# Row transposes of the second batch placed later, three ReLUs moved from ScalarE to VectorE, and transforms of later batches placed slightly earlier, in a retention + Fourier-mix + feed-forward kernel

## The chip, the cores and the metric

One core of a Trainium2 chip runs the whole kernel. The metric is device time of one execution in microseconds (us), median of several executions. A profiled execution also gives a span (first to last instruction, some 1.8 to 2.1 us less than the device time) and a record of every instruction. Batches, row blocks and hidden blocks are counted from 0: batch 1 is the second batch.

## The reference, cut to what matters

Four batches of 768 rows and 512 columns. Retention attention with a decaying state per head gives `x`; then a Fourier mix, a normalisation and a two-layer network:

```python
# q, k, v: (4, 8, 768, 64); w_ch1: 512 x 2048; w_ch2: 2048 x 512
state = gamma * state + k[t] (x) v[t]          # per head, over 768 steps
x[t]  = scale * q[t] @ state
u  = x + real(fft(fft(x, axis=1), axis=2))     # rows, then columns
un = (u - mean(u)) / sqrt(var(u) + 1e-6)
out = u + max(un @ w_ch1, 0) @ w_ch2
```

## The kernel before

The kernel works with two halves of 384 rows per batch; a row block is 128 rows. The feed-forward part of batch b is the bulk of TensorE's work. Woven between its units is the attention of batch b+1 and the mix of the next row half. The parts that the argument needs (cuts marked with `# ...`):

```python
ACT_ROWS = ((2, 4, 5, 6, 7, 8, 9, 10, 14), (0, 3, 6, 7, 9, 10, 11, 12, 14, 15), (2, 4, 5, 6, 7, 8, 9, 10, 14))

def h_unit(b, rt, fb):                    # hidden block fb of 16, row half rt
    psh = ps_pm.tile(...)                 # one of 3 PSUM buffers
    for cb in range(4):
        nc.tensor.matmul(psh, w116[...], unT[...])            # 4 x 384 columns
    if fb in ACT_ROWS[2 if (b, rt) == (B - 1, 0) else rt]:
        nc.scalar.activation(ht16[:, fb, :], psh, AF.Relu, ...)
    else:
        nc.vector.tensor_scalar(out=ht16[:, fb, :], in0=psh, ...)   # ReLU too

# second transform of row block kb ("pq"), from its unit:
pq = ps_g.tile(...)                       # the PSUM pool that wkK, wkA, wkY, pst use too
# ... 4 matmuls into pq
nc.scalar.copy(qn..., pq...)              # twice (L829, L830)
nc.vector.scalar_tensor_tensor(out=u[:, kb, 0:256], in0=lo, ...)     # L834, reads pq
nc.vector.scalar_tensor_tensor(out=u[:, kb, 256:512], in0=updn, ...) # L837, reads pq
nc.gpsimd.tensor_tensor(out=u[:, kb, 0:256], ...)       # + x, L864
nc.gpsimd.tensor_tensor(out=u[:, kb, 256:512], ...)     # + x, L866
nc.vector.bn_stats(bst, u[:, kb, :])                    # L883
# ... mean, then un = u - mean on ScalarE (L885)

def unT_unit(b, kb):                      # transposed rows, for h_unit
    if b > 1 or b and kb >= 3:
        nc.sync.dma_start_transpose(unT[...], un)       # by DMA
        return
    # else 4 transposes on TensorE ("pst"), copy on VectorE or ScalarE
```

Where a unit goes in the order is set by numbers, in fractions of a batch's work. A list of units is spread evenly between a start and an end, all lists are merged by that place, and a scheduler builds the final order for each engine from it:

```python
dm = (0.12, 0.24, 0.3, 0.38) if b == 0 else (0.004, 0.140, 0.232, 0.341)
streams += [(majors, b, b + 1.0), (s2s, b + dm[0], b + dm[1]),   # pq of row blocks 3 to 5
            (unTs, b + dm[2], b + dm[3])]                        # their transposes
# ... attention of batch b+1, ending at `end`
da = (0.062, 0.080, 0.173, 0.203, 0.255, 0.305) if b == 0 else \
    (0.068, 0.072, 0.053, 0.163, 0.173, 0.194)
streams.append((s1 units of b+1, end + da[0], end + da[1]))      # first transform
s2s, unTs = mix_units(b + 1, [0, 1, 2])
streams += [(s2s, end + da[2], end + da[3]), (unTs, end + da[4], end + da[5])]
```

## Time and profile before

| | before |
|---|---|
| device time, median of 3 | 248.96 us (248.73 to 249.09) |
| span of the profiled execution | 247.2 us |
| TensorE waits outside the start-up, turn to batch 1 / 2 / 3 | 2.01 / 1.11 / 1.20 us |

The last row is worked out in the prediction. From the list of waits of TensorE (engine, what waited and its line, what released it: total us, times, longest), two lines of the turns:

```profile
PE wkY L644 <- DVE u L837: 0.8, 2, 0.4
...
PE pst L914 <- ACT un L885: 0.4, 1, 0.4
```

These are gaps as shown; what a gap costs beyond that is worked out in the prediction. In timelines, a line is: start, length from first start to last end, engine, line, operation, output<-input, shape, count, and in brackets the gap before it with what ended it. PE is TensorE, DVE VectorE, ACT ScalarE and POOL GpSimd; L644 is line 644 of the kernel. The prediction explains most names; besides them, v is the cast of v to 16 bits, s the state update of the attention, atm its mask product, bst and stats the row statistics, and ob the output.

### The profile page before, as it was taken

What the parts mean: (1) busy time and instruction counts of PE and PEld (TensorE: products, weight loads), DVE (VectorE), ACT (ScalarE), POOL (GpSimd) and SP (SyncE); (2) the same over time, 40 slices, a digit from 0 to 9 for tenths busy, and PEclk for the clock granted to TensorE, in tenths of its full rate; (3) what the DMA queues carried; (4) which work ended last, traced back from release to release, by engine and by line L of the source; (5) the groups of instructions that cost most, each with busy time, mean ns of one, the idle gap of its engine ahead of it and who ended that gap; (6) DMA issues with size and microseconds to landing.
All of it is one profiled execution on the core that took longest, in us unless ns stands there. A gap on an engine that the chain in (4) does not pass through costs nothing.

```text
span 247.2 us, 5308 instructions
## 1 busy us (share of the span) xinstructions
PE 234.4 (95%) x2024; PEld 144.2 (58%) x2024; DVE 176.5 (71%) x427; ACT 124.8 (50%) x279; POOL 81.6 (33%) x146
## 2 busy tenths in 40 slices
PE   6797899999999999999999999999999998999994
PEld 2454668956776645665567546555666455445543
DVE  8988957898788787897885748787895656424112
ACT  8798678487786434651247515632257317202500
POOL 7668500385500075690000636760002314000000
PEclk9999999999999999999999999999999999999999
DMA  8999999699999288979999468685200241221012
GB/s 174 258 258 148 197 198 203 154 245 261 280 225 219 46 170 195 205 146 139 263 271 201 98 153 199 117 137 127 81 0 3 49 143 23 44 85 42 0 45 85
DMA packets 99209, 36.39 MB, mean 147 GB/s; under 512 B 89840, under 2 KB 96240, under 8 KB 99184
## 3 DMA queue, kind: packets, MB, share of 16 engines
q1 hardware_dynamic: 94960, 31.86, 61.4%
q0 software_dynamic: 4224, 4.19, 10.5%
q8 instruction: 16, 0.26, 0.4%
q14 instruction: 9, 0.07, 0.1%
HBM read 27.26 MB, written 6.29 MB: 136 GB/s over the span
## 4 chain that ended last, share of the span: by engine, by line
PE 66%; DVE 10%; POOL 8%; ACT 6%; SPq 3%; issue 2%; DMA 2%; POOLq 0%; DVEq 0%; ACTq 0%
PE psc L973 30%; PE psh L930 19%; PE ps L730 3%; SPq L159 3%; PE psh L947 3%; DVE bst L883 3%; POOL u L866 2%; DMA k<-in_k_dram 2%; POOL u L864 2%; PE wkA L594 2%; PE wkY L648 2%; DVE u L834 1%; DVE ht L936 1%; PE wkY L644 1%; PE tq L550 1%
## 5 line engine op out<-in xcount | busy, mean ns | idle before, releaser
L973 PE MATMUL psc<-w,ht 128*128 128x512 f16 (+1 forms) x400 | 89.8, 370 | 0.1
L930 PE MATMUL psh<-unT,w 128*128 128x384 f16 x448 | 81.9, 326 | 0.8 <-ACT ht L934 0.6
L973 PEld LDWEIGHTS <-ht 128*128 128x128 f16 x400 | 38.0, 98 | 35.3 <-issue 0.3
L930 PEld LDWEIGHTS <-w 128*128 128x128 f16 x448 | 42.2, 98 | 24.8 <-issue 2.0
L934 ACT ACTIVATE ht<-psh 128x384 f16<-128x384 f32 x67 | 31.6, 488 | 37.9 <-PE psh L930 37.1
L864 POOL TENSOR_TENSOR u<-u,x 128x256 f32<-128x256 f32 x21 | 13.3, 636 | 102.6 <-DVE u L834 92.2
L977 DVE SCALAR_TENSOR_TENSOR ob<-psc,stats,u 128x512 f32<-128x512 f32 (+1 forms) x25 | 18.1, 722 | 26.8 <-PE psc L973 26.7
L936 DVE TENSOR_SCALAR ht<-psh 128x384 f16<-128x384 f32 x45 | 24.7, 551 | 8.5 <-PE psh L930 7.9
L597 DVE TENSOR_TENSOR atm<-wkA,maskp 128x512 f16<-128x512 f32 x36 | 23.9, 683 | 1.0 <-PE wkA L594 1.0
L885 ACT ACTIVATE un<-u,stats 128x512 f16<-128x512 f32 x21 | 15.1, 721 | 18.5 <-DVE stats L884 14.8
L883 DVE BATCH_NORM_STATS2 bst<-u 128x6 f32<-128x512 f32 x21 | 14.6, 695 | 10.7 <-POOL u L866 10.5
L623 DVE SCALAR_TENSOR_TENSOR s<-s,gk,wkK 128x128 f16<-128x128 f16 x48 | 16.4, 342 | 2.5 <-ACT s L619 1.4
L656 ACT ACTIVATE x<-wkY,gexp 128x384 f16<-128x384 f32 x24 | 12.9, 581 | 8.3 <-PE wkY L648 8.3
L377 POOL TENSOR_SCALAR kd<-k,gexp 128x384 f16<-128x384 f32 x24 | 13.8, 587 | 2.5 <-DMA k<-in_k_dram 2.5
L145 PE MATMUL wps<-ht 128*128 128x512 f16 x40 | 12.6, 419 | 2.2 <-POOL ht L196 2.2
L866 POOL TENSOR_TENSOR u<-u,x 128x256 f32<-128x256 f32 x21 | 13.4, 636 | 3.6 <-DVE stats L884 1.8
L594 PE MATMUL wkA<-qTz,kT 128*128 128x256 f16 x72 | 13.6, 273 | 0.0
L829 ACT COPY qn<-pq 128x128 f32<-128x128 f32 x18 | 5.0, 275 | 14.6 <-PE pq L827 14.6
L947 PE MATMUL psh<-unT,w 128*128 128x128 f16 x192 | 11.5, 219 | 0.1
L947 PEld LDWEIGHTS <-w 128*128 128x128 f16 x192 | 11.1, 98 | 0.7 <-issue 0.5
L382 POOL TENSOR_SCALAR v<-v 128x768 f16<-128x768 f32 x12 | 10.0, 833 | 2.0 <-DMA v<-in_v_dram 1.9
L594 PEld LDWEIGHTS <-kT 128*128 128x128 f16 x72 | 6.9, 98 | 6.0 <-DVE s L623 0.4
(164 smaller groups left out, 318.8 us busy)
## 6 DMA issues: line engine op xcount, KB each, us to landing
q<-in_q_dram SPq DMA_DIRECT2D x16, 384.0 KB, 6.2
k<-in_k_dram SPq DMA_DIRECT2D x16, 384.0 KB, 5.6
v<-in_v_dram SPq DMA_DIRECT2D x16, 384.0 KB, 6.4
out_dram<-ob SPq DMA_DIRECT2D x23, 256.0 KB, 2.6
w<-in_moe_w_ch_dram POOLq DMA_DIRECT2D x8, 512.0 KB, 11.0
out_dram<-ob SPq DMA_DIRECT2D x2, 128.0 KB, 1.7
unT<-un SPq DMA_TRANSPOSE x15, 2.4
qTz<-q16z SPq DMA_TRANSPOSE x8, 3.8
```

The source lines that it names most:

```text
L594: mm = nc.tensor.matmul(wk[:, c2], st["kT"][:, c, :], st["qT"][:, :, c, :], start=True, stop=True)
L597: nc.vector.tensor_tensor(out=st["atm"][:, 2 * part:2 * part + 2], in0=wk, in1=maskp[:, PAIR_ORDER[i]].unsqueeze(1).to_broadcast([P, 2, 2, ...
L623: nc.vector.scalar_tensor_tensor(out=s16[:, c], in0=s16[:, c - 1], scalar=gk2[:, hp:hp + 1], in1=wk[:, c - c0], op0=ALU.mult, op1=ALU.add)
L864: nc.gpsimd.tensor_tensor(out=u[:, kb, 0:256], in0=u[:, kb, 0:256], in1=x[:, kb, 0, 1:257], op=ALU.add)
L866: nc.gpsimd.tensor_tensor(out=u[:, kb, 256:512], in0=u[:, kb, 256:512], in1=x[:, kb, 1, 257:1:-1], op=ALU.add)
L883: nc.vector.bn_stats(bst, u[:, kb, :])
L930: nc.tensor.matmul(psh, w116[:, cb, fb * P:(fb + 1) * P], unT[:, cb, rt * 384:(rt + 1) * 384], start=(cb == 0), stop=(cb == 3))
L934: nc.scalar.activation(ht16[:, fb, :], psh, AF.Relu, bias=0.0, scale=-1.0)
L936: nc.vector.tensor_scalar(out=ht16[:, fb, :], in0=psh, scalar1=-1.0, scalar2=0.0, op0=ALU.mult, op1=ALU.max)
L947: mm = nc.tensor.matmul(psh[:, f], w116[:, cb, fb * P:(fb + 1) * P], unT[:, cb, kb * P:(kb + 1) * P], start=(cb == 0), stop=(cb == 3))
L973: nc.tensor.matmul(psc[:, c0:c1], ht16[:, fb, rb3 * P:(rb3 + 1) * P], w216[:, fb, c0:c1], start=(fb == 0), stop=(fb == NFB - 1))
L977: nc.vector.scalar_tensor_tensor(out=ob[:, c0:c1], in0=psc[:, c0:c1], scalar=lb[b]["st"][:, rb, 3:4], in1=lb[b]["u"][:, rb, c0:c1], op0=AL ...
```

## The change

The description that came with it speaks of q of later batches on GpSimd, of row transposes of the second batch, and of ReLU shares placed anew. The diff has only numbers; nothing in it touches q or GpSimd:

```diff
-ACT_ROWS = ((2, 4, 5, 6, 7, 8, 9, 10, 14), (0, 3, 6, 7, 9, 10, 11, 12, 14, 15), (2, 4, 5, 6, 7, 8, 9, 10, 14))
+ACT_ROWS = ((2, 5, 6, 7, 8, 9, 10, 14), (0, 3, 6, 7, 9, 10, 11, 12, 14, 15), (2, 4, 5, 6, 7, 8, 10, 14))
...
-            da = (0.062, 0.080, 0.173, 0.203, 0.255, 0.305) if b == 0 else \
-                (0.068, 0.072, 0.053, 0.163, 0.173, 0.194)
+            da = (0.062, 0.080, 0.173, 0.203, 0.271, 0.321) if b == 0 else \
+                (0.063, 0.067, 0.048, 0.158, 0.168, 0.189)
```

## The prediction

> **What bounds the kernel now.** I read the page first (busy time, slices, chain, groups), then the list of waits of TensorE, then each engine's timeline where TensorE waited. Part 1 and the slices of the page:
>
> ```profile
> PE 234.4 (95%) x2024; PEld 144.2 (58%) x2024; DVE 176.5 (71%) x427; ACT 124.8 (50%) x279; POOL 81.6 (33%) x146
> ...
> PE   6797899999999999999999999999999998999994
> ```
>
> TensorE's records cover 234.4 of 247.2 us, and after the first quarter every slice but the last is near 9. The granted clock is full throughout. So the only time to win is what TensorE still waits. In the groups a 128x384 matmul's record lasts 326 ns, yet the chain of waits gives "0.65 PE psh L930 x4", 0.163 us each: the last 0.16 us of each record lies over the next matmul. A gap shown as 0.41 therefore costs about 0.57, and a wait under 0.16 doesn't show at all. Where I say "costs" below, it is this: distance between two starts, less 0.163 us (384 columns), 0.216 us (512 columns) or what else the shape takes in an unbroken run.
>
> (Names in the lines: psh and psc are the first and second matmul of the feed-forward part, ht its hidden values, un the normalised rows and unT their transposes, pq the second transform, u its sum, wkK, wkA and wkY the attention of the next batch.)
>
> Counted so, the waits outside the start-up (which the change doesn't touch) sit in three places, one at each turn from a batch to the next. TensorE's timeline there:
>
> ```profile
> 90.87 1.03 PE L973 MATMUL psc<-w,ht 128*128 128x512 f16 x4
> 92.30 0.40 PE L914 MATMUL pst<-ident,un 128*128 128x128 f16 x4 [0.41 <-ACT un L885]
> ...
> 94.09 0.40 PE L914 MATMUL pst<-ident,un 128*128 128x128 f16 x4
> ...
> 97.66 0.44 PE L613 MATMUL wkK<-v,kd 128*128 128x128 f16 x5
> ...
> 105.14 0.43 PE L644 MATMUL wkY<-s,qTz 128*128 128x64 f16 x9 [0.42 <-DVE u L837]
> ...
> 108.67 0.81 PE L930 MATMUL psh<-unT,w 128*128 128x384 f16 x4
> ...
> 157.97 0.44 PE L644 MATMUL wkY<-s,qTz 128*128 128x64 f16 x9 [0.42 <-DVE u L837]
> ...
> 206.72 2.11 PE L930 MATMUL psh<-unT,w 128*128 128x384 f16 x12 [0.21 <-ACT ht L934]
> 209.27 3.41 PE L930 MATMUL psh<-unT,w 128*128 128x384 f16 x20 [0.43 <-ACT ht L934]
> ```
>
> Batch 1: the second transpose waits for its normalised rows (0.57), the third too (0.26), the first unit of the hidden layer (psh) 0.08 for the third's copy; then wkY waits for a PSUM buffer that VectorE empties late (0.58), then for a mask product (0.21), and hidden units near 108.7 for VectorE's ReLUs (0.07 and 0.24). Together 2.01 us. Batch 2: the same four late waits, 0.59 + 0.21 + 0.07 + 0.24 = 1.11. Batch 3: hidden units wait for ScalarE's ReLUs, 0.38 and 0.60, then 0.22 for one of VectorE: 1.20. In all 4.3 us, 1.7% of the time: the change cannot win more than that unless the start-up changes too.
>
> **What the Trainium skill says.** Perfetto Trace Analysis, section "Identifying the Most-Contended Engine": matmul busy time says little of how near the roofline a kernel is, since matmuls are pipelined. The trace agrees: 326 ns records at a pace of 163. The same page, "Identifying Performance Opportunities", under its optimization strategy: take the gaps on that engine, find which semaphore they wait on, and make that dependency start sooner or finish faster. The change does this. PSUM — Partial Sum Buffer, section "The four PSUM rules": GpSimd cannot touch PSUM, so a ReLU out of PSUM taken from ScalarE can only go to VectorE; the trace has no PSUM operand on GpSimd. VectorE: DVE Perf Modes, section "Why PSUM operands drop a tier": an f32 PSUM operand runs in the plain mode. The trace fits: the ReLU out of PSUM takes 551 ns on VectorE (384 columns), 488 on ScalarE.
>
> **The change part by part.** No instruction is added or removed but by kind: three ReLUs (hidden block 4 of batches 1 and 2, block 9 of batch 3, each in the first row half) go from ScalarE to VectorE. Cost: 3 x 551 ns on VectorE (71% busy), 3 x 488 off ScalarE (50% busy). The words of the change speak of q on GpSimd; the diff has nothing of it, and the built order of GpSimd's instructions is the same. What else moves is order on TensorE, VectorE and ScalarE, which I read from the two built programs.
>
> Batch 1 (transposes of normalised rows 16 thousandths of a batch later). Built order now: 8 psc, transpose, 4 psc, transpose, 4 psc, transpose, 4 pq, 5 wkK, 4 pq, then the hidden units; before: 4, 4, 6 and 2 psc between them, and pq and wkK among the hidden units. The other engines' lines that decide:
>
> ```profile
> 91.53 0.72 ACT L885 ACTIVATE un<-u,stats 128x512 f16<-128x512 f32 x1 [1.10 <-DVE stats L884]
> 93.31 0.72 ACT L885 ACTIVATE un<-u,stats 128x512 f16<-128x512 f32 x1
> ...
> 94.12 0.83 POOL L382 TENSOR_SCALAR v<-v 128x768 f16<-128x768 f32 x1
> ...
> 94.53 0.42 DVE L919 COPY unT<-pst 128x512 f16<-128x512 f16 x1
> 94.96 0.75 DVE L977 SCALAR_TENSOR_TENSOR ob<-psc,stats,u 128x512 f32<-128x512 f32 x1
> ```
>
> First transpose at 90.64 + 4 x 0.216 = 91.51; second at 91.51 + 0.22 + 0.86 = 92.59, its rows being ready at 92.25: no wait. Third at 93.67 if ready; its mean is now computed on VectorE before the first unT copy, about 0.2 sooner, so its rows end at 93.8 and it starts at 93.87: cost 0.2. Then pq to 94.31. Then wkK, which is moved ahead of the hidden units, needs the v cast of GpSimd, and that ends at 94.12 + 0.83 = 94.95: cost 0.7. It hides the wait for the third unT copy, which now stands behind the ob of 0.75 us on VectorE and ends at about 95.3. wkK and pq from 95.0 to 95.49, hidden units from there. Before, they began at 95.00, but 0.05 + 0.27 + 0.22 = 0.54 us of pq and wkK were still to do. So the transposes' own gain, 0.91 less 0.9, is about nothing.
>
> What is gained comes after. The two pq are done at 94.3 and 95.5 in place of 96.4 and 98.8, so VectorE forms u of blocks 3 and 4 sooner, and GpSimd begins the second casts at about 97.0 in place of 98.80 and is free for u of block 4 at 99.9 in place of 101.69. I walked VectorE's built order with the measured times (ReLU 0.47 to 0.55 from start to start, statistics 0.61, s 0.26, mask product 0.59, u 0.4): the last u read of PSUM ends at about 103.8 in place of 105.1, the third mask product at 104.4 in place of 105.7. TensorE reaches wkY at about 104.6: the waits of 0.58 and 0.21 are gone. The ReLUs near 106 then come one place earlier between the state updates, so 0.07 and 0.24 go too: 1.10. Against it, eight hidden units now stand nearly unbroken with three PSUM buffers; block 4 waits about 0.16 for the ReLU of block 1, which stands behind a statistics instruction. Sum for batch 1: 2.01 before, 0.2 + 0.7 + 0.16 = 1.06 after, gain 0.95.
>
> Batch 2: TensorE's order there is unchanged. The added ReLU (0.47) falls into VectorE's wait for GpSimd:
>
> ```profile
> 154.51 0.64 POOL L864 TENSOR_TENSOR u<-u,x 128x256 f32<-128x256 f32 x1
> ...
> 155.78 0.69 DVE L883 BATCH_NORM_STATS2 bst<-u 128x6 f32<-128x512 f32 x1 [0.87 <-POOL u L866]
> ...
> 157.44 0.47 DVE L837 SCALAR_TENSOR_TENSOR u<-pq,g,qn 128x256 f32<-128x256 f32 x1
> ```
>
> Statistics at 155.78 wait 0.87 for GpSimd's sum, which itself stands behind the casts. Half the wait is filled, the start stays, and with it the PSUM read that ends at 157.92 and the wkY wait of 0.59 (and 0.21). Only the order of ReLUs and state updates near 160 is better: 0.24 + 0.07 less. Say 0.25.
>
> Batch 3: ScalarE normalises block 3 and 4 ahead of the ReLUs that TensorE waits for:
>
> ```profile
> 205.57 0.72 ACT L885 ACTIVATE un<-u,stats 128x512 f16<-128x512 f32 x1 [0.61 <-DVE stats L884]
> 206.20 1.23 ACT L934 ACTIVATE ht<-psh 128x384 f16<-128x384 f32 x3
> ...
> 208.12 0.72 ACT L885 ACTIVATE un<-u,stats 128x512 f16<-128x512 f32 x1 [0.35 <-issue]
> 208.75 1.23 ACT L934 ACTIVATE ht<-psh 128x384 f16<-128x384 f32 x3
> ```
>
> Block 5's ReLU ends at 206.7 and block 8's at 209.2 with or without block 9 behind them, as both stand behind the normalisation in the built order too. So 0.38 and 0.60 stay: gain 0.
>
> Second-stage transforms of batches 2 and 3 start 5 thousandths (0.26 us) earlier: the fourth ps is now issued before a hidden unit, and the pq after it may wait about 0.05 for ScalarE's copy of it, twice: loss 0.1. The stage had no waits.
>
> Sum: 0.95 + 0.25 + 0 - 0.1 = 1.1 us, so 248.96 - 1.1 = 247.86 us.
>
> **Rivals.** (a) The wait is only replaced: if VectorE, which takes the ReLU in its densest stretch, is later than I walked, wkY in batch 1 waits as before and the gain is 0.2 or less: 248.8. For it speaks that the same stretch in batch 2, with pq standing later, keeps its wait. Against it: GpSimd gets its u work some 1.8 us sooner. (b) All three turns are cured, as the ReLUs placed anew in batches 2 and 3 would suggest: 4.3 less the 1.06 left in batch 1: 245.7. Against it: the built orders of batches 2 and 3 leave the waits' causes where they were. (c) The transposes' third unit, moved ahead of the hidden layer, starves TensorE longer: wkK and the copy behind ob would cost more than 0.9. If the v cast slipped by 1 us: 248.9. GpSimd's lines before it, though, hang on work that comes before the first moved instruction, so I expect 94.95 again.
>
> **Range and chances.** Repeated times of the kernel before spread over 0.36 us. Of my terms the surest is that batch 3 stays, the least sure batch 1's VectorE walk (0 to 1.5). 8 in 10: 247.1 to 248.8. Over 2% faster would be 243.98, more than all the waits there are: 0.01. Slower by over 2% would take 5 us of new waits on an engine order that hardly changed: 0.01. Within 2%: 0.98.
>
> **What would show it.** In the trace of the changed kernel: no wait before the second transpose; a wait of about 0.5 shown before wkK, ended by GpSimd's v; no wait at wkY in batch 1 but still 0.42 in batch 2; 0.21 and 0.43 before hidden units in batch 3; hidden units after the turn to batch 1 starting near 95.5 and psc near 108.5 in place of 109.5. I am wrong if batch 1 still waits at wkY, or if batch 3's waits go.

## The result, and the profile after

The changed kernel takes 247.57 us (247.44 to 247.99, 4 runs) beside 248.87 us (248.73 to 249.09, 4 runs) before, in the same rounds. The ratio is 0.995, 95% interval 0.9933 to 0.9967. A ratio here is the mean time of one kernel's fast runs over that of the other's fast runs in the same rounds, so it is not quite the ratio of the medians quoted. The span fell from 247.2 to 246.0 us. Part 1 of the page:

```profile
PE 234.4 (95%) x2024; PEld 144.4 (59%) x2024; DVE 177.5 (72%) x430; ACT 124.3 (51%) x276; POOL 81.3 (33%) x146
```

Three instructions more on VectorE, three fewer on ScalarE: the ReLUs. TensorE's busy time is the same to the tenth, so the whole gain is waits. From its list of waits:

```profile
PE wkK L613 <- POOL v L382: 0.5, 1, 0.5
...
PE wkY L644 <- DVE u L837: 0.4, 1, 0.4
```

One of two wkY waits is gone, the wait for `un` is gone, and one for the v cast is new. TensorE's timeline shows where:

```profile
92.95 1.03 PE L973 MATMUL psc<-w,ht 128*128 128x512 f16 x4
94.03 0.40 PE L914 MATMUL pst<-ident,un 128*128 128x128 f16 x4
...
95.12 0.44 PE L613 MATMUL wkK<-v,kd 128*128 128x128 f16 x5 [0.47 <-POOL v L382]
...
95.63 4.77 PE L930 MATMUL psh<-unT,w 128*128 128x384 f16 x28
...
104.66 0.45 PE L644 MATMUL wkY<-s,qTz 128*128 128x64 f16 x10
...
156.97 0.44 PE L644 MATMUL wkY<-s,qTz 128*128 128x64 f16 x9 [0.36 <-DVE u L837]
...
208.03 3.41 PE L930 MATMUL psh<-unT,w 128*128 128x384 f16 x20 [0.44 <-ACT ht L934]
```

The third transpose comes at 94.03; with four psc at 0.216 us behind 92.95 it could have come at 93.81, so it cost 0.22. wkK cost 0.64. From 95.63 seven hidden units run almost without a gap, and at 104.66 all ten wkY of the first half run in one piece, where the kernel before stopped for 0.58 us.

Why wkY no longer waits is read on GpSimd and VectorE. From the timeline of all engines in the kernel before:

```profile
97.60 0.64 POOL L864 TENSOR_TENSOR u<-u,x 128x256 f32<-128x256 f32 x1 [2.65 <-DVE u L834]
...
101.69 0.63 POOL L864 TENSOR_TENSOR u<-u,x 128x256 f32<-128x256 f32 x1
...
102.95 0.69 DVE L883 BATCH_NORM_STATS2 bst<-u 128x6 f32<-128x512 f32 x1 [0.86 <-POOL u L866]
...
104.61 0.48 DVE L837 SCALAR_TENSOR_TENSOR u<-pq,g,qn 128x256 f32<-128x256 f32 x1
```

In the changed kernel:

```profile
95.83 0.63 POOL L864 TENSOR_TENSOR u<-u,x 128x256 f32<-128x256 f32 x1 [0.76 <-DVE u L834]
...
99.91 0.64 POOL L864 TENSOR_TENSOR u<-u,x 128x256 f32<-128x256 f32 x1
...
101.57 0.69 DVE L883 BATCH_NORM_STATS2 bst<-u 128x6 f32<-128x512 f32 x1
...
103.21 0.48 DVE L837 SCALAR_TENSOR_TENSOR u<-pq,g,qn 128x256 f32<-128x256 f32 x1
```

Row for row, every step is 1.4 to 1.8 us earlier. The last read of a pq (L837) frees the PSUM buffer that wkY wants. Before, it ended at 104.61 + 0.48 = 105.09, and wkY went on at 105.14; now it ends at 103.69, a full microsecond before TensorE gets to wkY.

Counted as in the prediction, the waits are 0.22 + 0.64 + 0.06 = 0.92 us in batch 1 (before: 2.01), 0.52 + 0.21 + 0.06 and a new one of 0.05 before a hidden unit near 152, together 0.84, in batch 2 (1.11), and 0.37 + 0.60 + 0.22 = 1.19 in batch 3 (1.20). That is 1.37 won; 0.13 was lost in the start-up of this execution, which the change doesn't touch (the same eight pq matmuls start at 86.73 before and at 86.86 now). 1.24 fits the 1.2 of the spans and the 1.3 of the medians.

### The profile page after: what moved, and what is told of

The parts are those of the page before. It is cut to its first block, busy times and chain, and to the rows that moved or that the text cites. A ratio compares the mean times of both kernels' runs of the same rounds, so it can differ in the third digit from the quotient of the medians.

```text
span 246.0 us, 5309 instructions
## 1 busy us (share of the span) xinstructions
PE 234.4 (95%) x2024; PEld 144.4 (59%) x2024; DVE 177.5 (72%) x430; ACT 124.3 (51%) x276; POOL 81.3 (33%) x146
## 4 chain that ended last, share of the span: by engine, by line
PE 72%; DVE 8%; POOL 7%; ACT 4%; SPq 3%; DMA 2%; issue 2%; POOLq 0%; DVEq 0%
PE psc L973 30%; PE psh L930 23%; SPq L159 3%; PE ps L730 3%; PE psh L947 3%; PE wkA L594 3%; DMA k<-in_k_dram 2%; PE wkY L648 2%; POOL u L864 2%; POOL u L866 2%; PE wkY L644 1%; DVE bst L883 1%; PE wkK L613 1%; DVE u L834 1%; PE pq L827 1%
## 5 line engine op out<-in xcount | busy, mean ns | idle before, releaser
L934 ACT ACTIVATE ht<-psh 128x384 f16<-128x384 f32 x64 | 30.6, 488 | 39.4 <-PE psh L930 38.3
L936 DVE TENSOR_SCALAR ht<-psh 128x384 f16<-128x384 f32 x48 | 26.3, 551 | 8.6 <-PE psh L930 8.3
L145 PE MATMUL wps<-ht 128*128 128x512 f16 x40 | 13.3, 439 | 2.2 <-POOL ht L196 2.2
```

What stands on the lines that cost most here:

```text
L934: nc.scalar.activation(ht16[:, fb, :], psh, AF.Relu, bias=0.0, scale=-1.0)
L936: nc.vector.tensor_scalar(out=ht16[:, fb, :], in0=psh, scalar1=-1.0, scalar2=0.0, op0=ALU.mult, op1=ALU.max)
```

## The experiments

The theory (A): batch 1's gain comes from the pq that move ahead of the hidden units along with the transposes; they feed VectorE, then GpSimd, then VectorE again, and so free wkY's buffer. The rivals: (B) the ReLU of block 4 clears the way, (C) the second-stage move wins something, (D) the transposes' own waits were the gain. D is hard to hold already from the trace above: 0.91 us of waits at the transposes before, 0.86 at the third transpose and wkK now. Every experiment has its own runs of the kernel before on the same chip; the intervals below are 95%.

| run | median us | before us | ratio to before (interval) |
|---|---|---|---|
| e1_transposes | 248.26 | 249.09 | 0.9965 (0.9951 to 0.9978) |
| e2_relus | 248.52 | 249.09 | 0.9975 (0.9962 to 0.9987) |
| e3_second_stage | 248.93 | 249.09 | 0.9991 (0.9977 to 1.0005) |
| e8_no_hoist | 247.88 | 249.09 | 0.9951 (0.9939 to 0.9964) |
| e10_no_hoist | 248.80 | 248.92 | 0.9992 (0.9979 to 1.0004) |
| e4_vcast_act | 248.13 | 248.92 | 0.9966 (0.9952 to 0.9979) |
| e5_pool_delay | 248.31 | 248.92 | 0.9972 (0.9960 to 0.9985) |
| e6_b3_late | 247.42 | 249.09 | 0.9938 (0.9925 to 0.9951) |
| x7a | 248.16 | 249.09 | 0.9968 (0.9954 to 0.9981) |
| x7b | 248.22 | 249.09 | 0.9975 (0.9957 to 0.9992) |
| e11_b3_mid | 246.67 | 249.02 | 0.9905 (0.9889 to 0.9922) |

### The transposes alone

```diff
 # the kernel before, with
-            da = (0.062, 0.080, 0.173, 0.203, 0.255, 0.305) if b == 0 else \
+            da = (0.062, 0.080, 0.173, 0.203, 0.271, 0.321) if b == 0 else \
```

> Only the transposes of batch 1 are moved; the three ReLUs stay on ScalarE and the second stage stays. Theory A (the gain of batch 1 comes from the two pq that move ahead of the hidden units with the transposes): 0.9 to 1.1 us faster than the kernel before, ratio about 0.996; wkY in batch 1 starts without a wait, wkK waits about 0.6 for the v cast. Rival B (it is the ReLU of block 4 that VectorE takes which clears the way): 0.3 us or less; wkY waits as before.

The fast runs gave 0.0035 x 249.09 = 0.87 us, near theory A and far from B.

> The transposes alone once more, only for a trace: the profiled execution of the first try lasted 481.8 us in a state of its own. Expected from its fast times (0.85 us under before): no wait at wkY in batch 1, wkK waits 0.6 us, batch 2 keeps its 1.1 us of waits and batch 3 its 1.2.

That single run took 248.50 us (state unknown, span 246.4). The wkY wait of batch 1 is gone with all ReLUs in their old place, which rules out B for that wait. But the ReLUs have their share elsewhere: a hidden unit of batch 1 now waits 0.58 us, where the kernel before lost 0.07 + 0.24. From the timeline of all engines in this run, in order of time:

```profile
106.50 1.10 DVE L623 SCALAR_TENSOR_TENSOR s<-s,gk,wkK 128x128 f16<-128x128 f16 x3
107.52 1.01 DVE L936 TENSOR_SCALAR ht<-psh 128x384 f16<-128x384 f32 x2
...
108.12 0.81 PE L930 MATMUL psh<-unT,w 128*128 128x384 f16 x4 [0.41 <-DVE ht L936]
```

Three state updates stand in one piece ahead of the ReLU that TensorE needs. In the changed kernel ReLUs and state updates alternate there, and nothing waits; VectorE's timeline:

```profile
105.59 0.53 DVE L936 TENSOR_SCALAR ht<-psh 128x384 f16<-128x384 f32 x1
106.03 0.34 DVE L623 SCALAR_TENSOR_TENSOR s<-s,gk,wkK 128x128 f16<-128x128 f16 x1
106.28 0.55 DVE L936 TENSOR_SCALAR ht<-psh 128x384 f16<-128x384 f32 x1
```

The transposes alone therefore leave batch 1 at 0.22 + 0.65 + 0.06 + 0.58 = 1.51 us: they win 0.5 of the 1.09. Batch 2 and the first two waits of batch 3 are as before.

### The ReLUs alone

```diff
 # the kernel before, with the new ACT_ROWS of the change and nothing else
```

> Only the three ReLUs go from ScalarE to VectorE; TensorE's order is that of the kernel before. Theory A: 0.2 to 0.4 us faster (batch 2's late waits of 0.24 and 0.07 shrink; in batch 1 VectorE has more to do in its densest stretch, so wkY still waits 0.5 or more). Rival B: 0.8 us faster or more.

It won 0.0025 x 249.09 = 0.62 us, between the two expectations. The trace has 1.79 us of waits in batch 1 (2.01 before): wkY still waits, 0.53 and 0.21, but the late waits are 0.06 where they were 0.07 and 0.24. Batch 2 has 0.53 + 0.21 + 0.06 and the new 0.05, together 0.85 (1.11 before), within 0.01 of what the whole change leaves there. So B is wrong for wkY; the late waits of 0.24, in both batches, are the ReLUs' work.

### The second stage alone

```diff
 # the kernel before, with
-                (0.068, 0.072, 0.053, 0.163, 0.173, 0.194)
+                (0.063, 0.067, 0.048, 0.158, 0.168, 0.189)
```

> Only the second-stage transforms of later batches start 5 thousandths earlier. My prediction had a loss of 0.1 us here (pq waiting for ScalarE's copy); the trace of the changed kernel shows none, so now: 0.0, within 0.15 us of the kernel before. Rival C (this move, too, wins part of the 1.2 us): 0.2 to 0.4 us faster.

0.0009 x 249.09 = 0.22 us, with an interval that holds zero. In the trace all waits of batches 1 and 2 are those of the kernel before, and the stage itself has no new wait: my loss of 0.1 us was wrong. One wait is missing, the 0.22 us before the first psc of batch 3. It is missing in the traces of all three single parts and present in the kernel before and in the changed one, though the built order there is the same in the second-stage run and before. ScalarE's last normalisation of batch 3 starts 2.7 us after the one ahead of it in the single parts and 3.0 in the other two. By the semaphore records of the traces, everything that it waits for has come 0.16 us before its start in the single parts and 0.44 before it in the other two, so what holds it the extra 0.28 us is no recorded wait for another engine or a transfer; its cause stays open. It also makes the parts add up to more than the whole (0.87 + 0.62 + 0.22 = 1.71 us against 1.3); thrice 0.22 of it is this wait.

### Early pq undone, first try

```diff
 # the changed kernel, with
-            da = (0.062, 0.080, 0.173, 0.203, 0.271, 0.321) if b == 0 else \
+            da = (0.062, 0.080, 0.173, 0.203, 0.275, 0.315) if b == 0 else \
```

> The changed kernel with the transposes of batch 1 at 0.275 and 0.315 in place of 0.271 and 0.321: in the built order they still come later than before, but the second follows the first at once, and pq and wkK go back among the hidden units as in the kernel before; all other parts of the change stay. Theory A: most of batch 1's gain is lost, 0.7 to 1.1 us slower than the changed kernel, some 0.2 to 0.5 faster than before; wkY in batch 1 waits again. Rival B (the ReLUs) or D (the transposes' own waits): 0.4 us or less of the gain is lost, no wait at wkY.

0.9951: as fast as the changed kernel, which looks like a refutation of A. It isn't one. The trace shows pq and wkK ahead of the hidden units as in the changed kernel, and a fresh build shows the changed kernel's order on every engine. I had read the order from listings of several builds made at once, and they had evidently been mixed up. The run says nothing of A; it is a second measurement of the changed kernel, on the chip of the three runs above, and the one to compare them with.

### Early pq undone, second try

```diff
 # the changed kernel, with
-            da = (0.062, 0.080, 0.173, 0.203, 0.271, 0.321) if b == 0 else \
+            da = (0.062, 0.080, 0.173, 0.203, 0.271, 0.313) if b == 0 else \
```

> The changed kernel with the transposes of batch 1 at 0.271 and 0.313 (third one 8 thousandths earlier). Order on TensorE, from a fresh build: third transpose directly behind the second, then four psc, then hidden units, with pq and wkK among the hidden units as in the kernel before. The third transpose must wait about 1.0 us for its rows, which replaces the 0.2 and 0.65 us of the changed kernel, so TensorE has done equally much by 95.5 us; only the order of pq and wkK differs after it. Theory A (early pq carries batch 1's gain): the wkY wait of 0.5 and the mask product's 0.2 come back, 0.6 to 0.9 us slower than the changed kernel, that is ratio to before about 0.998. Rival D (the waits went because of the transposes and ReLUs themselves): no wait at wkY, ratio 0.995.

The gain is gone: 0.9992. TensorE's timeline in this run:

```profile
94.01 0.40 PE L914 MATMUL pst<-ident,un 128*128 128x128 f16 x4 [0.91 <-ACT un L885]
...
96.41 0.39 PE L827 MATMUL pq<-gk,g16r 128*128 128x129 f16 x4
...
98.87 0.39 PE L827 MATMUL pq<-gk,g16r 128*128 128x129 f16 x4
...
105.42 0.44 PE L644 MATMUL wkY<-s,qTz 128*128 128x64 f16 x9 [0.36 <-DVE u L837]
```

ReLUs and second stage are those of the changed kernel, the first two transposes too. The two pq come at 96.41 and 98.87 where the changed kernel has them at 94.26 and near 95.4, and wkY waits again, 0.53 and then 0.21 for the mask product. The third transpose waits 1.08, which is 0.22 more than the 0.86 of third transpose and wkK that it replaces, so the 1.0 us that was lost (0.9992 less 0.9951, of 249) is about 0.7 for the late pq and 0.2 for the transpose. Theory A holds, with one limit: wkK goes back together with the pq, and no run parts the two. That it is the pq that hold the chain up is read from GpSimd: in this run it stands idle 2.82 us, until 97.89, for the first of these u, and the statistics at 103.23 then wait 0.45 for its sum. D falls: the three transposes start within 0.02 us of where they do in the changed kernel, and nothing is won.

### The v cast that wkK waits for

```diff
 # the changed kernel, with
+                if (b, i) == (2, 0):
+                    last_cast[b, i] = nc.scalar.copy(v16, v32...)
+                else:
                     last_cast[b, i] = nc.gpsimd.tensor_scalar(out=v16, in0=v32..., ...)
```

> The changed kernel with the v cast that wkK waits for (batch 2, first pair) on ScalarE in place of GpSimd, ahead of the second unT copy. My reading in the prediction: the 0.64 us wait hides the wait for the unT copies, which end near 95.4, so hidden units start at most 0.2 us earlier and the gain is 0.0 to 0.2 us over the changed kernel. Rival E (the wait is a true loss): 0.5 to 0.6 us faster than the changed kernel, ratio to before about 0.9925.

wkK's wait shrank from 0.64 to 0.26, yet the kernel became about 0.4 us slower than the changed one (0.9966 against 0.9951). Counted from the first transpose, hidden units start 95.20 - 91.39 = 3.81 us later, against 95.63 - 91.64 = 3.99 in the changed kernel: 0.18 won, within the 0.0 to 0.2 of my reading. What takes the place of wkK's wait is one of 0.2 before the second pq, which starts at 94.97: by the trace's semaphores it waits for ScalarE's copy of a transpose, which now stands behind the cast and ends at 94.92. The 0.6 of the rival is not there. What I hadn't seen is the price, in the timeline of all engines:

```profile
95.48 0.48 DVE L837 SCALAR_TENSOR_TENSOR u<-pq,g,qn 128x256 f32<-128x256 f32 x1 [0.64 <-ACT qn L833]
...
98.51 2.11 PE L933 MATMUL psh<-unT,w 128*128 128x384 f16 x12 [0.55 <-DVE ht L939]
```

The cast holds ScalarE up for 0.8 us, so its copy of pq is late, VectorE stands idle for 0.64 before u, and the ReLU behind it makes a hidden unit wait 0.71 in place of 0.06.

### GpSimd delayed

```diff
 # the changed kernel, with
+                for _ in range(3 if (b, i) == (2, 1) else 1):
                     last_cast[b, i] = nc.gpsimd.tensor_scalar(out=v16, in0=v32..., ...)
```

> The changed kernel with the second v cast of batch 2 on GpSimd done three times (1.6 us more of GpSimd work ahead of u of block 4; nothing else waits for it soon). Theory F (in batch 1 the last u read of PSUM is paced by GpSimd, through the statistics that stand ahead of it on VectorE): wkY waits again, 0.5 us or more, and the kernel is 0.4 to 1.0 us slower than the changed one. Rival G (VectorE's own work paces it, GpSimd has slack): within 0.2 us of the changed kernel.

0.9972, some 0.5 us slower than the changed kernel. In the timeline of all engines:

```profile
102.50 0.69 DVE L884 BATCH_NORM_STATS2 bst<-u 128x6 f32<-128x512 f32 x1 [1.24 <-POOL u L867]
...
104.16 0.47 DVE L838 SCALAR_TENSOR_TENSOR u<-pq,g,qn 128x256 f32<-128x256 f32 x1
...
104.69 0.44 PE L645 MATMUL wkY<-s,qTz 128*128 128x64 f16 x9 [0.23 <-DVE u L838]
```

Same order on TensorE and VectorE, only GpSimd 1.6 us busier: the statistics wait for its sum, the pq read behind them ends at 104.63, wkY starts at 104.69. That makes waits of 0.40 and 0.21. Theory F holds: the chain to wkY in this turn runs through GpSimd, and this shows why the early pq help. The wkY wait alone is shorter than the 0.5 expected, for the changed kernel had slack there.

### Batch 3's transforms later

```diff
 # the changed kernel, with
+        if b == 3:
+            dm = (0.28, 0.36, 0.40, 0.44)
```

> The changed kernel with batch 3's second transforms of the second row half moved later, into the psc part (0.28 to 0.44 of the batch in place of 0.004 to 0.232), so that no normalisation stands among the ReLUs of its sixteen hidden units. Theory H (batch 3's waits of 0.37, 0.60 and 0.22 come from ScalarE normalising rows ahead of ReLUs): these waits go, 0.8 to 1.2 us faster than the changed kernel, ratio to before about 0.991. Rival I (the work only moves: psc or the later hidden units wait for the rows instead): within 0.3 us of the changed kernel.

All three waits of batch 3 are gone, 1.19 us: its hidden units run in one piece, for no normalisation stands among ScalarE's ReLUs. The move takes VectorE's and GpSimd's part of the transforms away too, but the traces of both kernels end the two large waits by a ScalarE ReLU that stands behind a normalisation, so for these theory H's cause is right; the third, of 0.22, came and went with the build. But the ratio is 0.9938, only some 0.3 us better than the changed kernel, since a new wait of 0.71 has come:

```profile
221.31 7.00 PE L930 MATMUL psh<-unT,w 128*128 128x384 f16 x42 [0.55 <-DMA unT<-un]
```

The next row half's hidden units wait for the last transposed rows, which come by DMA, 2.4 us from issue to landing. Rival I had this half right.

### Batch 2's transforms spread, too

```diff
 # as the run before, and for x7a / x7b
+        if b == 2:
+            dm = (0.004, 0.240, 0.270, 0.380)    # x7a
+            dm = (0.020, 0.190, 0.250, 0.360)    # x7b
```

> As e6_b3_late, and batch 2's second transforms spread over 0.004 to 0.240 of the batch, transposes 0.270 to 0.380: the last pq stands behind wkY. If batch 2's wait at wkY (0.52 and 0.21) comes from the u read of PSUM on VectorE that wkY's buffer waits for, it goes: another 0.4 to 0.8 us faster, ratio to before 0.988 to 0.990. Rival: the later rows delay the second half's hidden units, no gain over e6_b3_late.

> As x7a with batch 2's second transforms over 0.020 to 0.190 and transposes 0.250 to 0.360: a middle way. Expected between e6_b3_late and x7a: 0.989 to 0.991.

Both missed: 0.9968 and 0.9975, slower than without it. In x7a the wkY wait near 157 is gone as intended, but six microseconds later mask products, late behind the u that I had moved, make wkY wait 0.66, 0.64 and 0.57. In x7b wkY still waits 0.56 near 156, now for a mask product, and a hidden unit waits 1.31 for a ReLU of VectorE. TensorE's timeline in x7a:

```profile
162.92 0.19 PE L644 MATMUL wkY<-s,qTz 128*128 128x64 f16 x1 [0.50 <-DVE atm L597]
```

What one place wins, a place behind it pays. VectorE is not simply full there: just ahead of the late ReLU of x7b it stands idle 1.23 us, until its statistics at 159.29 have GpSimd's sum.

### Batch 3's transforms less late

```diff
 # the changed kernel, with
+        if b == 3:
+            dm = (0.28, 0.33, 0.38, 0.42)
```

> As e6_b3_late, with batch 3's second transforms and transposes less late (0.28 to 0.33, 0.38 to 0.42): the second and third pq stand four psc earlier each, 0.86 us. In e6_b3_late the next row half's hidden units waited 0.72 us for the last transposed rows. If theory H is right and that wait was the whole of what gave its gain back, the wait shrinks to under 0.2 and the kernel is 0.4 to 0.7 us faster than e6_b3_late, ratio to before 0.991 to 0.992. If the rows are held by VectorE's queue and not by pq (rival), the wait stays near 0.5 and the ratio near 0.993 to 0.994.

246.67 us, ratio 0.9905: 2.35 us under the kernel before in medians and, by the ratios (0.9905 against 0.9951), about 1.1 us under the changed one. The fastest kernel. TensorE's timeline:

```profile
199.77 9.91 PE L930 MATMUL psh<-unT,w 128*128 128x384 f16 x60
...
220.67 5.54 PE L930 MATMUL psh<-unT,w 128*128 128x384 f16 x33
```

The matmuls of all sixteen hidden units run in one piece (64 of them; the window of this view cuts the first four and the end of the second line off), and the second half starts without a shown gap (0.10 us by the count). The wait for the DMA was indeed what the first version had given back: it shrank by 0.61 us, and the span by 0.6 (245.4 to 244.8).

## Why the prediction was right

It said 247.86 us, a gain of 1.1; it is 247.57, a gain of 1.3. Every sign that it named came, wkK's wait for v and the unchanged gaps of batch 3 among them; the gap at wkY in batch 2 came as 0.36 and not 0.42.

- **Batch 1, 0.95 us.** Measured 1.09. The terms of what is left: third transpose 0.2 (0.22), wkK on the v cast 0.7 (0.64), hidden block 4 0.16 (0.06; seven hidden units stand in one piece, not eight). "The transposes' own gain is about nothing" and "what is gained comes after" were right: with the transposes later but pq (and wkK) late again, the gain is gone. The walk through GpSimd and VectorE came out within 0.1 us (second casts at 97.0, u of block 4 at 99.9, last PSUM read at 103.8 against 103.7).
- **The last two waits of batch 1 (0.07 and 0.24).** The size was right, and so was the order that it read (ReLUs one place earlier between the state updates); what brings that order was put in the wrong place, among the gains of the early pq. With the transposes alone these waits grow to 0.58; with the ReLUs alone they shrink to 0.06. The block moved off ScalarE makes the scheduler alternate ReLUs and state updates. The two parts of the change need each other: 0.5 and 0.22 us of batch 1 alone, 1.09 together.
- **Batch 2, 0.25 us.** Measured 0.27, by the ReLUs, as said: the wkY wait stays (0.52 where 0.59 stood), the late 0.24 goes, and the new 0.05 comes.
- **Batch 3, 0.** Measured 0.01; the ReLU of block 9 changes none of the three waits. The cause of the two large ones, ScalarE's normalisations ahead of ReLUs, was shown by moving them away. The 0.22 depends on a delay whose cause is open.
- **Second stage, -0.1.** Wrong: no new wait in the changed kernel's trace or in the part alone.
- **Rivals.** (a) and (c) needed a later VectorE or a later v cast; neither came. (b), all turns cured, fails on batch 2 and 3 as argued.

The terms erred in the same small way: 0.14, 0.02 and 0.1 us too cautious, with 0.13 lost in the start-up of the profiled execution. The range, 1.7 us wide, held with room to spare.

## What to carry to other kernels

When one instruction waits long and the ones before it can be put in another order, ask not how the wait itself can be shortened but what else gets ahead by it: here the removed wait was paid back at once by two others (0.86 us), and the gain came 10 us later, through two other engines. Look for work whose results feed such a chain, and put it in front of work that has slack, but check by a fresh build which order came out, since a step of 0.008 in a placement number flipped it. Where several engines wait for one another in turn, moving one unit may only move the wait (x7a, x7b); where an engine is only badly ordered, as ScalarE was in batch 3, moving its work to a stage with idle room wins nearly the whole wait, provided that the transfer behind it still lands in time.

## What the Trainium skill lacked or had wrong

- "TensorE: Matmul & The Clock Gate", section "Back-to-back issue gap", gives about 131 ns per matmul of 512 columns as what a stream sustains, and calls its formula (216 ns) an over-count there. The runs show the formula: four psc of the fastest kernel, between two pq, start at 209.75 and are followed at 210.61, so they take 0.86 us, 0.215 each, and 0.163 us for 384 columns throughout.
- "DMA: Bandwidth & Descriptors", section "DMA Transpose (X-bar)", gives constraints and no time from issue to landing of a transpose. Here a 128x512 transpose of 2-byte values within SBUF took 2.4 us (3.1 for one of three in the run with batch 3's transforms later), and that set the end of a wait.
- No page says outright that a shown TensorE gap understates a wait. Here it does, by the 0.16 us by which the record of a 384-column matmul (326 ns) exceeds its pace (163 ns); the gap of 0.47 before wkK cost 0.64.
